# Moving the narrowing, bounds and splits of the second network's weights one stage ahead

## The chip, the cores and the metric

One core of a Trainium2 chip. The metric is the device time in microseconds (us) of one execution of the whole program, the median of several runs. Engines are called as the profile calls them: PE (TensorE matmuls), PEld (its weight loads), DVE (VectorE), ACT (ScalarE), POOL (GpSimd), SP (SyncE, which issues all the DMAs).

## The reference

Attention whose mask allows only pairs of query and key that fall to the same centroid, then two feed-forward networks on 1536 tokens of 512 features:

```python
h = np.maximum(x @ w1[e], 0.0); out += p[:, e:e + 1] * (h @ w2[e])   # 4 experts, 512 -> 1024 -> 512
h = x @ w_in; g = np.maximum(0.01 * h, h); out = g @ w_out           # 512 -> 2048 -> 512
```

The weights of the experts are float32. Those of the second network (w_in, w_out) come as float64.

## The kernel before

After attention the two networks are done in 24 chunks of 256 hidden columns, here called stages 0 to 23: stages 0 to 15 are the experts (N1 = 16), 16 to 23 the second network. A stage has two phases. The **product phase** makes h = x @ w1 for its 256 columns, applies the activation and splits h in two (hhi by ACT, hlo = g - hhi by POOL). The **output phase** makes h @ w2 in twelve **tiles** of six matmuls (emit_y1 or emit_y2), each into a PSUM bank of its own; DVE adds each tile to the accumulator. Every fp32 matmul is done as three fp16 ones on a high and a low part (hi·hi, hi·lo, lo·hi).

Stages 0 to 2 and 16 to 18 (PLAIN) do the product phase as six blocks of twelve matmuls. The others use seven products of half-size blocks in place of eight (emit_seven); for that, sums of the four blocks of w1 (tile `sums`, fp32, made by POOL, split into shi and slo) and sums of blocks of x are kept. In emit_seven DVE's additions (`plus`) stand between products that use the same PSUM bank: the last product adds onto bank d only after DVE has read d for c22.

Each weight chunk goes this way, w1 as part 0, w2 as part 1:

- **load**: SP moves it to raw12[part] (float32), or to raw64[part] for the second network (one buffer for each part).
- **narrow** (float64 only): five steps that build a float32 in raw12[part]; step 1 is an Abs on ACT, steps 2 to 5 are bit operations on DVE (L244, L247, L250, L253).
- **peak** (L216): ACT takes the largest absolute value of each partition. **peak_across** (L220): one small PE matmul into a PSUM bank brings the 128 values together. **peak_top** (L224 and `power`): DVE reduces them and makes a power of two. **out_scale** (L232) makes the factor for the output.
- **split** (weights_split): ACT scales raw12[part] in place (L267) and makes the high half (L260); POOL makes the low half in two instructions (L263).

raw12, w1hi/w1lo, w2hi/w2lo, raw64, sums, shi/slo are single buffers. Order on each engine is the order of emission (a manual schedule); each engine works through its queue in order, and waits between engines follow from the tiles that instructions read and write. Lists of small steps (`steps`, `later`, `late`) are spread over the blocks, products and tiles of a stage by popping a few after each.

In before, narrowing of w2 for stage c+1 starts with step 1 at the end of stage c's product phase (`late`, or the head of the output phase), steps 2 to 5 run between the first tiles of the output phase, and the peak after them. Its peak_across, peak_top and split run in the middle of the next stage's product phase. For w1 of stage c+1, steps 2 to 5 and the peak run in stage c's product phase, peak_across after tile 1, and peak_top and the split some tiles later. Bank 0 takes the peak_across of w1 after tile 1 and is wanted again by tile 6 (y_bank).

Stage 15 and 16 are the seam: stage 15's output phase also brings x for the second network into range (turn_sum, turn_max, turn_scale, turn_split: ACT and DVE), and stage 15 narrows both weights of stage 16. Attention ends with a list of actions sorted by a due time in sixths of a head (`at(when, fn)`); PEAK_AT holds the due times of the peaks of stage 0's two weights, FILL those of h products of stage 0 that are done early. `big()` hands out three PSUM tiles of two banks in turn.

Of the kernel before, what the change touches and what calls it, by code (L numbers as in the profile page):

```python
# [52 lines left out]
NORM_LAST = (6.49, 6.57)  # L53
PHI_LAST = ((0, 2, 4), (0, 2, 4))
SPLIT_AT = (2.3, 3.6, 5.3)
PEAK_AT = ((4.6, 7.2), (18.1, 19.0))
FILL = ((0, 0, 1.07), (0, 6, 1.08), (0, 12, 6.38), (0, 18, 6.39), (1, 0, 9.94), (1, 6, 10.27), (1, 12, 10.27))

BIG = float(2 ** 60)
# [17 lines left out]
def attention_moe_kernel(  # L77
# [13 lines left out]
    nc = tc.nc  # L91
# [120 lines left out]
        )  # L212
        nc.vector.reciprocal(out=t[:, 3:4], in_=t[:, 2:3])

    def peak(part):
        nc.scalar.activation(out=junk, in_=raw12[part].rearrange("p a b -> p (a b)"), func=AF.Abs, accum_out=pb16[part])  # L216

    def peak_across(part, ps):
        spread[part] = ps
# [16 lines left out]
    def weights_narrow(c, part):  # L236

        w = raw64[part].rearrange("p k (f t) -> p k f t", t=2)
        low, high = w[:, :, :, 0], w[:, :, :, 1]
        f = raw12[part]  # L240
        fi = f.bitcast(I32)
        return [
            lambda: nc.scalar.activation(out=f, in_=high.bitcast(F32), func=AF.Abs),
            lambda: nc.vector.tensor_scalar(  # L244
                out=f, in0=f, scalar1=F64_LEAST, scalar2=F64_MOST, op0=ALU.max, op1=ALU.min,
            ),
            lambda: nc.vector.tensor_scalar(  # L247
                out=fi, in0=fi, scalar1=3, scalar2=0x3FFFFFFF, op0=ALU.logical_shift_left, op1=ALU.bitwise_and,
            ),
            lambda: nc.vector.scalar_tensor_tensor(  # L250
                out=fi, in0=high, scalar=-0x40000000, in1=fi, op0=ALU.bitwise_and, op1=ALU.bitwise_or,
            ),
            lambda: nc.vector.scalar_tensor_tensor(  # L253
                out=fi, in0=low, scalar=29, in1=fi, op0=ALU.logical_shift_right, op1=ALU.bitwise_or,
            ),
        ]
# [7 lines left out]

    def weights_split(c, part, lo_engine=None):
        hi, lo = (w1s, w2s)[part][0]
        nc.scalar.activation(out=raw12[part], in_=raw12[part], func=AF.Copy, scale=pk[part][:, c % 2, 3:4])  # L267
        if lo_engine:
            split(hi, lo, raw12[part], lo_engine)
        else:  # L270
            split_halves(hi, lo, raw12[part])
# [564 lines left out]
        weights_load(0, 1)  # L836

    def peak_early(part):
        peak_across(part, big())
        peak_top(0, part)  # L840

    def split_early(n):
# [14 lines left out]
    def at(when, fn, *args):  # L857
        line.append((when, len(line), fn, args))
# [73 lines left out]
        at(when, warm, 1)  # L932
    at(J * (NH - 3) + 0.5, open_early)
    for part in range(2):
        at(J * (NH - 3) + PEAK_AT[part][0], peak, part)
        at(J * (NH - 3) + PEAK_AT[part][1], peak_early, part)
    for n in range(3):
        at(J * (NH - 2) + SPLIT_AT[n], split_early, n - 1)
# [128 lines left out]
                    like(ps, rhs), lhsT=w[:, k, fs], rhs=rhs, start=k + i == 0, stop=k == KC - 1 and i == 2,  # L1067
                )

    def emit_seven(c, steps):  # L1070

        w = w1s[0]
        a11, a12, a21, a22 = [
# [48 lines left out]
        for m in some_b:  # L1122
            product(z[m, "a"], a11, x11, m)
            nc.scalar.activation(out=u2[m], in_=z[m, "a"], func=AF.Copy)
        if not is_wide(c):
            weights_split(c, 1)
            out_scale(c)
        some()
        if c >= N1:
            plain_b(0)  # L1130
# [1 line left out]
        for m in some_b:  # L1132
            product(z[m, "b"], s2, t2, m)
            plus(u2[m], z[m, "b"], u2[m])
        if is_wide(c):
            peak_across(1, bank(7))
            peak_top(c, 1)
            weights_split(c, 1)
            out_scale(c)
        some()  # L1140
        for m in some_b:
            product(z[m, "a"], a12, x21, m, False)
# [11 lines left out]
        for m in some_b:  # L1154
            product(z[m, "e"], a22, t4, m)
            plus(z[m, "e"], z[m, "e"], u3[m])
            if m == A and c < N1:
                done(m, 1, 0, z[m, "e"])
            product(z[m, "d"], s1, t1, m)
            plus(c22[m], z[m, "d"], u3[m])  # L1160
        done(B if c < N1 else A, 1, 0, z[B if c < N1 else A, "e"])
        some()
        h_act(c, g, g, pbuf[0][:, 0, HT:HT + 512])
        split(hbuf[0][0][:, 1, HT:HT + 512], hbuf[0][1][:, 1, HT:HT + 512], g, nc.gpsimd)
        if c < N1:
            done(B, 1, 1, c22[B])
        else:
            plain_b(1)
        for m in some_b:
            product(z[m, "d"], s4, x22, m, False)  # L1170
            plus(z[m, "d"], z[m, "d"], u2[m])
            done(m, 0, 1, z[m, "d"])

    def emit_y1(c, i):

# [91 lines left out]
    for c in range(NCH):  # L1267
# [2 lines left out]
        steps, left, late = [], [], []  # L1270
        if more and is_wide(c + 1):
            narrow = [[] if c + 1 == N1 else weights_narrow(c + 1, n) for n in range(2)]
            if c == N1:
                steps.append(narrow[0][0])
            steps += narrow[0][1:]
            if c + 2 < NCH:
                steps.append(lambda: weights_load(c + 2, 0))
            steps.append(lambda: peak(0))
            if c + 1 == N1:
                steps += weights_narrow(N1, 1)  # L1280
            else:
                late.append(narrow[1][0])
        elif more:
            steps += [lambda: peak(0), lambda: weights_load(c + 1, 1)]
        if c in PLAIN:
            if not is_wide(c):
                weights_split(c, 1, nc.vector if c == 0 else None)
                out_scale(c)
            if c == N1:
                sums_left = turn_sums()  # L1290
                quota = [0, 0, 7, 0, 3, 3]
            if c == 0:
                sums_left = input_sums()
                quota = [0, 3, 7, 0, 5, 3]
            n = quota.pop(0)
            slots = mixed(sums_left[:n], steps) + late
            sums_left = sums_left[n:]
            if c == N1:
                turn_max(1)
                for k in range(KC):  # L1300
                    turn_split(1, k)
            blocks = [(u, f) for u in range(2 if c == 0 else 0, NU) for f in range(NF)]
            for n, (u, f) in enumerate(blocks):
                if c > 0 and c != N1:
                    ps = bank(BANKS[u][f])
                    plain(c, u, f, ps)
                elif f == 0:
                    both_ps = [bank(BANKS[u][f]) for f in range(NF)]
                    for k in range(KC):
                        for g in range(NF):  # L1310
                            plain(c, u, g, both_ps[g], [k])
                if c == 0 or c == N1:
                    ps = both_ps[f]
                h_whole(c, f, ps, 512 * u, hl=[tokens(x[:, f], c, u, True) for x in hbuf[0]])
                if c == N1 and (u, f) == (0, 1):
                    turn_across(1, bank(1))
                    turn_scale(1)
                    for k in range(KC):
                        turn_split(2, k)
                if is_wide(c) and (u, f) == (0, 1):  # L1320
                    peak_across(1, bank(6))
                    peak_top(c, 1)
                    weights_split(c, 1)
                    out_scale(c)
                if c == N1 and n < 2:
                    continue
                for _ in range(-(-len(slots) // (len(blocks) - n))):
                    slots.pop(0)()
        else:
            emit_seven(c, steps)  # L1330
            left = steps + late

        steps, later = left, []
        if c in PLAIN:
# [1 line left out]
            later, sums_left = sums_left[:n], sums_left[n:]  # L1336
        if more:
            if not is_wide(c + 1):
                later.insert(0, lambda: peak(1))
            else:  # L1340
                if c + 1 == N1:
                    steps.append(lambda: peak(1))
                else:
                    later += narrow[1][1:] + [lambda: peak(1)]
                if c + 2 < NCH:
                    later.append(lambda: weights_load(c + 2, 1))
            if L1_POINT(c):
                steps.append(lambda: weights_split(c + 1, 0))
            else:
                steps += [None, None, lambda: (peak_top(c + 1, 0), weights_split(c + 1, 0))]  # L1350
            if c + 1 not in PLAIN:
                steps += weights_sums()
            if c + 2 < NCH and not is_wide(c + 2):
                steps.append(lambda: weights_load(c + 2, 0))
# [9 lines left out]
        for i in range(NTILE):  # L1364
            (emit_y1 if c < N1 else emit_y2)(c, i)
            if i == 1 and more and not L1_POINT(c):
                peak_across(0, bank(0))
            if i == 8 and more and not is_wide(c + 1):
                peak_across(1, bank(7))
                steps.append(lambda: peak_top(c + 1, 1))  # L1370
            for _ in range(2 if c == N1 - 1 else -(-len(steps) // (NTILE - i))):
                step = steps.pop(0) if steps else None
                if step:
                    step()
        if c >= N1 and c + 2 < NCH:
            weights_narrow(c + 2, 0)[0]()


# [30 lines left out]
```

## Time and profile before

| | |
|---|---|
| median of 3 runs | 1002.84 us (1002.62 to 1002.92) |
| the profiled execution | 1002.35 us, of which the span from first to last instruction is 1000.6 |
| mean granted TensorE clock | 0.988 |
| PE busy | 957.6 us, 96% of the span |
| DVE, ACT, POOL busy | 730.5 (73%), 517.0 (52%), 534.3 (53%) |
| chain that ended last | PE 76%, DVE 11%, ACT 7%, POOL 3% |

A row of a timeline is: start, duration, engine, line, operation, output <- inputs with shapes, count, and in brackets how long the engine was idle before it and what ended that. A granted clock of 1.00 is full speed.

### The profile page before, as it was taken

How to read it: one execution, taken by the hardware profiler on the slowest of the kernel's cores; microseconds unless marked ns; L12 is line 12 of the kernel's file. 1: busy time of each engine (PE TensorE's matmuls, PEld its weight loads, DVE VectorE, ACT ScalarE, POOL GpSimd, SP SyncE). 2: the span in 40 equal slices, each digit the busy share in tenths (PEclk: the TensorE clock that was granted, in tenths of full speed). 3: DMA queues.
4: the chain of work that ended last, by engine and by line, in shares of the span. 5: the costliest groups of instructions: out<-in, count | busy, mean ns of one | idle time of the engine just before them, and what ended most of it. 6: DMA issues, size and time to landing. Idle time of an engine off the chain costs nothing.

```text
span 1000.6 us, 16132 instructions
## 1 busy us (share of the span) xinstructions
PE 957.6 (96%) x6347; PEld 547.9 (55%) x6380; DVE 730.5 (73%) x1264; ACT 517.0 (52%) x731; POOL 534.3 (53%) x444
## 2 busy tenths in 40 slices
PE   8899999997999999999999999999897999999998
PEld 5688888876444555555555555555443444434443
DVE  7988998887586767666666666667767967666654
ACT  3678877785443533443443444344573565455542
POOL 4477777760254656554565654455423746454543
PEclk9999999999999999999999999999899999999999
DMA  7875666430011031011301102131102122121103
GB/s 170 199 165 120 147 136 140 105 102 23 22 43 42 22 74 43 22 43 43 74 22 43 43 22 74 43 126 36 50 1 84 43 85 84 43 84 42 43 1 127
DMA packets 59540, 70.80 MB, mean 71 GB/s; under 512 B 25060, under 2 KB 42088, under 8 KB 59464
## 3 DMA queue, kind: packets, MB, share of 16 engines
q1 hardware_dynamic: 59464, 69.77, 26.4%
q8 instruction: 50, 0.82, 0.4%
q14 instruction: 26, 0.21, 0.1%
HBM read 46.19 MB, written 3.17 MB: 49 GB/s over the span
## 4 chain that ended last, share of the span: by engine, by line
PE 76%; DVE 11%; ACT 7%; POOL 3%; issue 2%; DMA 0%; DVEq 0%; ACTq 0%; POOLq 0%
PE z L1055 19%; PE z L1185 8%; PE z L1186 8%; PE z L1187 7%; PE z L1066 6%; PE z L1242 3%; PE z L1243 3%; PE z L1244 3%; PE big L510 3%; PE big L545 3%; PE big L546 2%; DVE m L514 2%; PE z L1114 2%; PE small L571 1%; PE small L572 1%
## 5 line engine op out<-in xcount | busy, mean ns | idle before, releaser
L141 POOL TENSOR_TENSOR hlo<-g,hhi 128x512 bf16<-128x512 f32 x140 | 175.9, 1272 | 131.8 <-ACT hhi L140 131.8
L1195 DVE SCALAR_TENSOR_TENSOR acc<-z,outer,acc 128x512 f32<-128x512 f32 x180 | 134.2, 749 | 75.2 <-PE z L1187 75.2
L559 POOL TENSOR_TENSOR plo<-p,phi 128x768 f16<-128x768 f32 x84 | 138.0, 1654 | 71.3 <-ACT phi L558 43.2
L1185 PE MATMUL z<-hhi,w2hi 128*128 128x512 f16 x384 | 145.8, 380 | 2.4 <-DVE pk L224 0.8
L140 ACT ACTIVATE hhi<-g 128x512 f16<-128x512 f32 x140 | 86.7, 628 | 116.4 <-DVE g L789 114.9
L1186 PE MATMUL z<-hhi,w2lo 128*128 128x512 f16 x384 | 145.8, 380 | 0.8 <-DVE w2lo L141 0.8
L1187 PE MATMUL z<-hlo,w2hi 128*128 128x512 bf16 x353 | 134.0, 380 | 0.0
L263 POOL TENSOR_TENSOR w2lo<-w2raw,w2hi 128x512 f16<-128x512 f32 x46 | 56.6, 1251 | 113.6 <-ACT w2hi L260 113.0
L514 DVE TENSOR_REDUCE m<-big 128x1 f32<-128x768 f32 x96 | 89.8, 950 | 14.5 <-PE big L510 14.2
L548 ACT ACTIVATE p<-big 128x768 f32<-128x768 f32 x96 | 77.4, 808 | 37.3 <-PE big L546 31.3
L263 POOL TENSOR_TENSOR w1lo<-w1raw,w1hi 128x512 f16<-128x512 f32 x46 | 56.1, 1241 | 75.3 <-ACT w1hi L260 48.9
L1242 PE MATMUL z<-w2hi,hhi 128*128 128x512 f16 x192 | 75.4, 393 | 7.3 <-DVE pk L224 7.3
L1251 DVE SCALAR_TENSOR_TENSOR accn<-z,outer,accn 128x512 f32<-128x512 f32 x84 | 61.1, 745 | 27.0 <-PE z L1244 27.0
L1066 PE MATMUL z<-xx,w1hi 128*128 128x512 f16 x256 | 76.3, 379 | 0.3 <-DVE xx L613 0.3
L1243 PE MATMUL z<-w2lo,hhi 128*128 128x512 f16 x192 | 75.4, 393 | 1.1 <-POOL w2lo L263 1.1
L1244 PE MATMUL z<-w2hi,hlo 128*128 128x512 f16 x192 | 75.3, 392 | 0.0
L545 PE MATMUL big<-qka 128*128 128x512 f32 x192 | 70.9, 370 | 2.9 <-DVE m L514 1.8
L1055 PEld LDWEIGHTS <-shi 128*128 128x128 f16 x496 | 48.8, 98 | 41.7 <-issue 5.9
L789 DVE SCALAR_TENSOR_TENSOR g<-z,pb 128x512 f32<-128x512 f32 x92 | 52.4, 576 | 20.1 <-PE z L1055 10.2
L1055 PE MATMUL z<-xx,shi 128*128 128x512 f16 (+1 forms) x248 | 62.7, 341 | 3.9 <-DVE g L1094 3.9
L1094 DVE TENSOR_TENSOR part<-z,part 128x512 f32<-128x512 f32 (+1 forms) x62 | 34.8, 578 | 41.3 <-PE z L1055 28.1
L573 PE MATMUL small<-vt,plo 128*128 128x65 f16 x576 | 61.0, 192 | 2.9 <-DVE plo L559 2.0
(238 smaller groups left out, 2263.8 us busy)
## 6 DMA issues: line engine op xcount, KB each, us to landing
qkb<-pair SPq DMA_DIRECT2D x32, 384.0 KB
w1raw<-in_moe_w_dram SPq DMA_DIRECT2D x16, 512.0 KB
w2raw<-in_moe_w_dram SPq DMA_DIRECT2D x16, 512.0 KB
w1raw<-in_moe_w_in_dram SPq DMA_DIRECT2D x8, 1024.0 KB
w2raw<-in_moe_w_out_dram SPq DMA_DIRECT2D x8, 1024.0 KB
qka<-pair SPq DMA_DIRECT2D x16, 384.0 KB
vraw<-in_v_dram SPq DMA_DIRECT2D x16, 192.0 KB
pb<-pe_rows SPq DMA_DIRECT2D x4, 768.0 KB
```

The costliest lines, as they stand in the source:

```text
L141: lo_engine.tensor_tensor(out=lo, in0=src, in1=as_read(hi), op=ALU.subtract)
L263: nc.gpsimd.tensor_tensor(out=lo[:, x], in0=src[:, x], in1=hi[:, x], op=ALU.subtract)
L514: nc.vector.tensor_reduce(out=m_t[t][:, j:j + 1], in_=ps[:, 0:S], op=ALU.max, axis=AX.X)
L559: (nc.vector if plo_on_vector else nc.gpsimd).tensor_tensor(out=plo, in0=p, in1=phi, op=ALU.subtract)
L1055: nc.tensor.matmul(ps, lhsT=w[i][:, k, :], rhs=x[j][:, k, sub], start=first and k + i + j == 0, stop=k == 1 and i == 1, skip_group_check=True,
L1066: nc.tensor.matmul(like(ps, rhs), lhsT=w[:, k, fs], rhs=rhs, start=k + i == 0, stop=k == KC - 1 and i == 2,)
L1185: nc.tensor.matmul(out, lhsT=whi[:, f, ks], rhs=h, start=f == 0, stop=False)
L1186: nc.tensor.matmul(out, lhsT=wlo[:, f, ks], rhs=h, start=False, stop=False)
L1187: nc.tensor.matmul(out, lhsT=whi[:, f, ks], rhs=l, start=False, stop=f == NF - 1)
L1195: nc.vector.scalar_tensor_tensor(out=a, in0=out, scalar=by, in1=a, op0=ALU.mult, op1=ALU.add)
L1242: nc.tensor.matmul(ps, lhsT=hi[:, f, ts], rhs=whi[:, f, :], start=f == 0, stop=False)
L1243: nc.tensor.matmul(ps, lhsT=hi[:, f, ts], rhs=wlo[:, f, :], start=False, stop=False)
```

## The change

- Due time of the peak matmul of stage 0's w2: 21.0 in place of 19.0; it uses the PSUM tile small0 in place of the next big tile.
- w2 of stage 16 is narrowed into `sums`; its peak is taken there, and its scaling writes raw12[1] from there.
- In stages 16 to 22 all five narrowing steps of the next w2 are in the product phase (`late`); its peak follows tile 1 of the output phase, its peak_across tile 8 (tile 5 in stage 15). Its split stands at the head of the next stage: in emit_seven after the first product, in stages 17 and 18 before the blocks, in stage 16 behind the second turn_split.
- peak_top and split of the next w1 follow peak_across directly, after tile 1.
- Narrowing steps 1 to 3 of w1 of stage 17 move to tiles 7 and 11 of stage 15. The peak of w1 comes before the load of the next w1.
- One of the block sums of x moves from stage 0's output phase to stage 1 (`quota`).

```diff
-PEAK_AT = ((4.6, 7.2), (18.1, 19.0))
+PEAK_AT = ((4.6, 7.2), (18.1, 21.0))
...
+    def narrowed(c, part):
+
+        return sums.rearrange("p (a e) b c -> p a (e b c)", a=2) if is_wide(c) and (c, part) == (N1, 1) else raw12[part]
...
     def weights_split(c, part, lo_engine=None):
         hi, lo = (w1s, w2s)[part][0]
-        nc.scalar.activation(out=raw12[part], in_=raw12[part], func=AF.Copy, scale=pk[part][:, c % 2, 3:4])
+        src = narrowed(c, part) if c else raw12[part]
+        nc.scalar.activation(out=raw12[part], in_=src, func=AF.Copy, scale=pk[part][:, c % 2, 3:4])
...
     def peak_early(part):
-        peak_across(part, big())
+        peak_across(part, small(0) if part else big())
         peak_top(0, part)
...
-    def emit_seven(c, steps):
+    def emit_seven(c, steps, late):
...
         for m in some_b:
             product(z[m, "a"], a11, x11, m)
             nc.scalar.activation(out=u2[m], in_=z[m, "a"], func=AF.Copy)
-        if not is_wide(c):
-            weights_split(c, 1)
-            out_scale(c)
+        weights_split(c, 1)
+        out_scale(c)
         some()
...
             product(z[m, "b"], s2, t2, m)
             plus(u2[m], z[m, "b"], u2[m])
-        if is_wide(c):
-            peak_across(1, bank(7))
-            peak_top(c, 1)
-            weights_split(c, 1)
-            out_scale(c)
         some()
...
             plus(c22[m], z[m, "d"], u3[m])
+        if late:
+            late[0]()
         done(B if c < N1 else A, 1, 0, z[B if c < N1 else A, "e"])
         some()
         h_act(c, g, g, pbuf[0][:, 0, HT:HT + 512])
         split(hbuf[0][0][:, 1, HT:HT + 512], hbuf[0][1][:, 1, HT:HT + 512], g, nc.gpsimd)
+        for step in late[1:3]:
+            step()
...
             done(m, 0, 1, z[m, "d"])
+        for step in late[3:]:
+            step()
...
             narrow = [[] if c + 1 == N1 else weights_narrow(c + 1, n) for n in range(2)]
-            if c == N1:
-                steps.append(narrow[0][0])
-            steps += narrow[0][1:]
-            if c + 2 < NCH:
-                steps.append(lambda: weights_load(c + 2, 0))
-            steps.append(lambda: peak(0))
+            load = [lambda: weights_load(c + 2, 0)] if c + 2 < NCH else []
             if c + 1 == N1:
-                steps += weights_narrow(N1, 1)
+                two = weights_narrow(N1, 1)
+                steps += [two[0], lambda: peak(c + 1, 0)] + load + two[1:]
             else:
-                late.append(narrow[1][0])
+                steps += narrow[0][3 if c == N1 else 1:] + [lambda: peak(c + 1, 0)] + load
+                late = narrow[1]
...
-                quota = [0, 3, 7, 0, 5, 3]
+                quota = [0, 2, 7, 1, 5, 3]
             n = quota.pop(0)
-            slots = mixed(sums_left[:n], steps) + late
+            slots = mixed(sums_left[:n], steps)
+            slots[len(slots) // 2:len(slots) // 2] = late[:1]
+            slots += late[1:]
             sums_left = sums_left[n:]
             if c == N1:
                 turn_max(1)
                 for k in range(KC):
                     turn_split(1, k)
+                weights_split(c, 1)
...
-                if is_wide(c) and (u, f) == (0, 1):
-                    peak_across(1, bank(6))
-                    peak_top(c, 1)
-                    weights_split(c, 1)
                     out_scale(c)
...
-                    later += narrow[1][1:] + [lambda: peak(1)]
+                    later.insert(0, lambda: peak(c + 1, 1))
...
-                steps += [None, None, lambda: (peak_top(c + 1, 0), weights_split(c + 1, 0))]
+                steps.insert(0, None)
...
             if i == 1 and more and not L1_POINT(c):
                 peak_across(0, bank(0))
-            if i == 8 and more and not is_wide(c + 1):
+                peak_top(c + 1, 0)
+                weights_split(c + 1, 0)
+            if i == (5 if c == N1 - 1 else 8) and more:
                 peak_across(1, bank(7))
                 steps.append(lambda: peak_top(c + 1, 1))
...
+            if c == N1 - 1 and is_wide(N1 + 1):
+                ahead = weights_narrow(N1 + 1, 0)
+                if i == 7:
+                    ahead[0]()
+                if i == 11:
+                    ahead[1]()
+                    ahead[2]()
```

## Rows read from the trace of the kernel before

**Rows 1.** Windows of stages 16, 17, 19, 22: us, busy (PE PEld DVE ACT POOL), clock, DMA.

```profile
730.62:771.22 40.60, 33.53 (x149) 14.63 (x148) 29.73 (x48) 25.77 (x42) 15.15 (x10) 0.96 0.12 36
771.22:802.41 31.19, 31.19 (x147) 14.19 (x146) 27.50 (x35) 17.91 (x24) 19.26 (x10) 1.00 0.21 68
833.60:867.56 33.96, 31.86 (x142) 13.97 (x140) 21.73 (x37) 19.58 (x28) 17.56 (x18) 0.95 0.28 93
935.49:966.73 31.24, 30.18 (x141) 13.54 (x140) 21.44 (x35) 15.58 (x23) 16.23 (x16) 1.00 0.00 1
```

**Rows 2.** PE's waits in the whole span, by releaser: total us, times, longest.

```profile
PE z L1242 <- DVE pk L224: 7.3, 4, 2.1
PE z L220 <- ACT junk L216: 5.6, 1, 5.6
PE z L1055 <- DVE g L1094: 3.9, 1, 3.9
...
PE big L220 <- ACT junk L216: 2.5, 1, 2.5
...
PE z L1243 <- POOL w2lo L263: 1.1, 2, 0.8
...
PE z L1185 <- DVE pk L224: 0.8, 1, 0.8
```

**Rows 3.** Windows of PE alone: length, busy, granted clock, DMA.

```profile
240.90:244.10 3.20, 3.19 (x9) 0.50 0.00 0
710.06:715.20 5.14, 5.14 (x16) 0.50 0.33 84
756.60:759.70 3.10, 3.10 (x9) 0.52 0.95 309
858.20:862.00 3.80, 3.80 (x11) 0.55 0.25 68
955.90:959.00 3.10, 2.04 (x10) 1.00 0.00 0
```

**Rows 4.** Timeline of DVE at the end of attention.

```profile
240.81 1.83 DVE L559 TENSOR_TENSOR plo<-p,phi 128x768 f16<-128x768 f32 x2
```

**Rows 5.** Timelines of ACT and DVE, product phase of stage 15.

```profile
700.04 1.04 ACT L216 ACTIVATE junk<-w1raw 128x1024 bf16<-128x1024 f32 x1
...
702.51 1.15 ACT L243 ACTIVATE w2raw<-w2raw 128x1024 f32<-128x1024 f32 x1 [1.34 <-POOL w2lo L263]
...
703.69 0.69 DVE L244 TENSOR_SCALAR w2raw<-w2raw 128x1024 f32<-128x1024 f32 x1 [4.70 <-ACT w2raw L243]
...
706.76 1.24 DVE L250 SCALAR_TENSOR_TENSOR w2raw<-w2raw,w2raw 128x1024 int32<-128x1024 int32 x1
```

**Rows 6.** Timelines of DVE and ACT, output phase of stage 15.

```profile
715.10 0.43 DVE L789 SCALAR_TENSOR_TENSOR g<-z,pb 128x256 f32<-128x256 f32 x1
...
719.96 0.75 DVE L1195 SCALAR_TENSOR_TENSOR acc<-z,outer,acc 128x512 f32<-128x512 f32 x1 [0.54 <-PE z L1187]
...
722.70 1.06 ACT L260 ACTIVATE w1hi<-w1raw 128x1024 f16<-128x1024 f32 x1
```

**Rows 7.** Chain that ended last, in order of time: start, us, what.

```profile
833.60 1.29 PE z L1055 x6
```

**Rows 8.** Timelines of POOL and DVE, apart and side by side, stages 14 and 16.

```profile
678.48 4.52 POOL L141 TENSOR_TENSOR hlo<-g,hhi 128x512 bf16<-128x512 f32 x4 [1.30 <-ACT hhi L140]
...
735.72 2.74 DVE L613 SCALAR_TENSOR_TENSOR xx<-acc,gx,xx 128x512 f16<-128x512 f32 x4 [0.46 <-ACT xx L612]
...
740.46 3.18 DVE L613 SCALAR_TENSOR_TENSOR xx<-acc,gx,xx 128x512 f16<-128x512 f32 x4 [1.18 <-ACT xx L612]
...
748.99 7.36 POOL L141 TENSOR_TENSOR hlo<-g,hhi 128x512 bf16<-128x512 f32 x4
...
751.18 2.06 DVE L250 SCALAR_TENSOR_TENSOR w1raw<-w1raw,w1raw 128x1024 int32<-128x1024 int32 x1
```

**Rows 9.** Timeline of POOL, product phase of stage 19.

```profile
842.70 2.53 POOL L263 TENSOR_TENSOR w2lo<-w2raw,w2hi 128x512 f16<-128x512 f32 x2 [2.68 <-ACT w2hi L260]
```

More of the change, by code (lines that the diff above doesn't have):

```diff
@@ L213, in power, with peak @@
         nc.vector.reciprocal(out=t[:, 3:4], in_=t[:, 2:3])
-    def peak(part):
-        nc.scalar.activation(out=junk, in_=raw12[part].rearrange("p a b -> p (a b)"), func=AF.Abs, accum_out=pb16[part])
+    def narrowed(c, part):
+        return sums.rearrange("p (a e) b c -> p a (e b c)", a=2) if is_wide(c) and (c, part) == (N1, 1) else raw12[part]
+    def peak(c, part):
+        src = narrowed(c, part) if c else raw12[part]
+        nc.scalar.activation(out=junk, in_=src.rearrange("p a b -> p (a b)"), func=AF.Abs, accum_out=pb16[part])
     def peak_across(part, ps):
@@ L239, in weights_narrow @@
         low, high = w[:, :, :, 0], w[:, :, :, 1]
-        f = raw12[part]
+        f = narrowed(c, part)
         fi = f.bitcast(I32)
@@ L266, in weights_split @@
         hi, lo = (w1s, w2s)[part][0]
-        nc.scalar.activation(out=raw12[part], in_=raw12[part], func=AF.Copy, scale=pk[part][:, c % 2, 3:4])
+        src = narrowed(c, part) if c else raw12[part]
+        nc.scalar.activation(out=raw12[part], in_=src, func=AF.Copy, scale=pk[part][:, c % 2, 3:4])
         if lo_engine:
@@ L934, in attention_moe_kernel @@
     for part in range(2):
-        at(J * (NH - 3) + PEAK_AT[part][0], peak, part)
+        at(J * (NH - 3) + PEAK_AT[part][0], peak, 0, part)
         at(J * (NH - 3) + PEAK_AT[part][1], peak_early, part)
@@ L1272, in attention_moe_kernel @@
             narrow = [[] if c + 1 == N1 else weights_narrow(c + 1, n) for n in range(2)]
-            if c == N1:
-                steps.append(narrow[0][0])
-            steps += narrow[0][1:]
-            if c + 2 < NCH:
-                steps.append(lambda: weights_load(c + 2, 0))
-            steps.append(lambda: peak(0))
+            load = [lambda: weights_load(c + 2, 0)] if c + 2 < NCH else []
             if c + 1 == N1:
-                steps += weights_narrow(N1, 1)
-            else:
-                late.append(narrow[1][0])
+                two = weights_narrow(N1, 1)
+                steps += [two[0], lambda: peak(c + 1, 0)] + load + two[1:]
+            else:
+                steps += narrow[0][3 if c == N1 else 1:] + [lambda: peak(c + 1, 0)] + load
+                late = narrow[1]
         elif more:
-            steps += [lambda: peak(0), lambda: weights_load(c + 1, 1)]
+            steps += [lambda: peak(c + 1, 0), lambda: weights_load(c + 1, 1)]
         if c in PLAIN:
-            if not is_wide(c):
+            if c != N1:
                 weights_split(c, 1, nc.vector if c == 0 else None)
@@ L1311, in attention_moe_kernel @@
                             plain(c, u, g, both_ps[g], [k])
[L1312 to L1315, printed above, removed]
+                if c == N1 and n == 0:
                     turn_across(1, bank(1))
@@ L1319, in attention_moe_kernel @@
                         turn_split(2, k)
-                if is_wide(c) and (u, f) == (0, 1):
-                    peak_across(1, bank(6))
-                    peak_top(c, 1)
-                    weights_split(c, 1)
                     out_scale(c)
+                if c == 0 or c == N1:
+                    ps = both_ps[f]
+                h_whole(c, f, ps, 512 * u, hl=[tokens(x[:, f], c, u, True) for x in hbuf[0]])
                 if c == N1 and n < 2:
@@ L1328, in attention_moe_kernel @@
                     slots.pop(0)()
+            left = []
         else:
-            emit_seven(c, steps)
-            left = steps + late
+            emit_seven(c, steps, late)
+            left = steps
         steps, later = left, []
@@ L1338, in attention_moe_kernel @@
             if not is_wide(c + 1):
-                later.insert(0, lambda: peak(1))
+                later.insert(0, lambda: peak(c + 1, 1))
             else:
                 if c + 1 == N1:
-                    steps.append(lambda: peak(1))
+                    steps.append(lambda: peak(c + 1, 1))
                 else:
-                    later += narrow[1][1:] + [lambda: peak(1)]
+                    later.insert(0, lambda: peak(c + 1, 1))
                 if c + 2 < NCH:
@@ L1374, in attention_moe_kernel @@
                     step()
-        if c >= N1 and c + 2 < NCH:
+            if c == N1 - 1 and is_wide(N1 + 1):
[5 more added lines that the diff above has]
+                    ahead[2]()
+        if c >= N1 and c + 2 < NCH and is_wide(c + 2):
             weights_narrow(c + 2, 0)[0]()
```

## The prediction

> **What bounds the kernel.** The table above says that PE is busy for 957.6 of 1000.6 us, so the time is PE's matmuls, PE's waits, and what the matmuls lose at a lower clock. I read the windows by stage first [rows 1]: stages 17 and 22 show PE busy all or nearly all the time, 31.19 of 31.19 and 30.18 of 31.24 us, and are the measure of an undisturbed stage; stages 16 and 19 are longer than PE's work in them. Then PE's waits by releaser [rows 2]: the six that touch this change sum to 7.3 + 5.6 + 3.9 + 2.5 + 1.1 + 0.8 = 21.2 us, and all name the peak, narrowing or splitting of weights, or DVE sums queued behind a narrowing step. Last, the granted clock behind those waits [rows 3]: it falls to its lower level (1.2 of 2.4 GHz) after the waits of 2 us and more, and stays at 1.00 after one of 1.06 us (955.90:959.00, PE busy 2.04 of 3.10). One minus the clock, times the stretch, is the loss: 1.6, 2.6, 1.5, and 1.7 in each of stages 19 to 21, which are alike: 10.8 us. So 32.0 us can be won at most, which would be 970.4 of the profiled execution's 1002.35.
>
> **What the change does to the count of work.** Nothing is added or removed: the same narrowings, peaks, splits and loads run, in another order, with one other buffer and one other PSUM tile. Every microsecond is a wait that goes or comes.
>
> **A. Hand-over from attention, and stage 0.** PE waited 2.5 us for the peak of the first w2 and then lost 1.6 to the clock [rows 2, 3]. The peak's matmul now stands behind twelve h products and three products with v. The h products take the next of the three big tiles, whose last reader, an exponential, is long done, so they start at once, 2.6 us of work at full clock. The v products then need the last plo, which DVE finishes at 240.81 + 1.83 = 242.64 [rows 4]; PE gets there at about 241.4 and waits 1.2. The shifted tiles also put the second block's h in the PSUM that stage 0 opens with: I allow 0.5 for it (0 to 1.4). 2.5 + 1.6 - 1.2 - 0.5 = 2.4. In stage 0 peak_top now follows tile 1 directly, so bank 0 is free for tile 6 and the 0.8 us wait goes. A gives 3.2 (1.0 to 4.9).
>
> **B. Stage 15.** Before, the first narrowing step of w2(16), the Abs on ACT, waited for POOL's split of the old weight in the same buffer and ended at 703.66; DVE, in order, stood behind it from 699.0 to 703.69, and the sums behind DVE's steps came late: the last product waited 3.9 us, to 710.06, then ran 5.1 us at half clock [rows 3, 5]. With the block-sum buffer the Abs takes the place of the peak at 700.04 and ends near 701.2, so DVE starts 2.45 sooner. The order on DVE from there to the c22 sum is unchanged, so PE resumes at 710.06 - 2.45 = 707.6; it is there at 706.2 and waits 1.4. That is nearer the 1.06 that left the clock alone than the 2 us that didn't: I take no loss (bound: the 2.6 stays). 3.9 + 2.6 - 1.4 = 5.1.
> Then a new wait. The peak of w2(16) must now be there after tile 5. DVE leaves the product phase 5.5 us after PE resumed (715.10 + 0.43 against 710.06), runs two accumulations and the scale chain, then ACT scales and splits w1: from an accumulation's start to the split's end is 719.96 to 723.76, 3.8; the extra accumulation is 0.7, the peak and its read-out 1.2 [rows 5, 6]. 5.5 + 0.7 + 3.8 + 1.2 = 11.2 after PE resumes. PE is at the end of tile 5 after 1.9 (the two last products) + 6 x 1.29 = 9.7, six matmuls of 512 columns taking 1.29 [rows 7]. So it waits about 1.4. B gives 3.7 (1.3 to 6.4). The Abs of w1(17) at tile 7 lies in ACT's idle time; the two DVE steps at tile 11 fall where DVE waits for ACT anyway: 0.
>
> **C. Stage 16.** Before: 1.1 for w2lo, 5.6 for the peak of w1(17), 1.5 of clock: 8.2 us [rows 2, 3]. Three of its five narrowing steps are now done in stage 15, and the split of w2(16) goes ahead of the blocks on ACT and POOL. DVE is free for steps 4 and 5 when the last splits of x end, at 740.46 + 3.18 = 743.6 in before's times, where step 4 began at 751.18 [rows 8]. Alone, two steps of 1.2 each and the peak would be done by about 747.5. PE asks for it two tiles into the output phase, 730.62 + 16.2 (six blocks of twelve matmuls, and 0.7 of small ones and waits) + 2.6 = 749.4: nothing would be left. But POOL is now busy in the same stretch. POOL's four subtractions took 4.52 us alone and 7.36 beside narrowing steps, one of which took 2.06 there and 1.24 alone; four x splits took 2.74 alone and 3.18 where they met POOL's for a moment [rows 5, 8]. That is taking turns, each waiting for the other. From 740.4 DVE has 5.0 us of such work (four x splits, two steps) and 0.4 that is free of POOL, and POOL has w2lo and three hlo to do all the while. Taking turns, the steps end at 740.4 + 2 x 5.0 + 0.4 = 750.8, the peak at 752.0; PE waits 2.6 and then loses 1.7 to the clock. C gives 8.2 - 4.3 = 3.9 (0.5, if POOL holds the steps another 3 us, to 8.2, if nothing is left). I take the 3.9, since each such DVE row beside POOL is stretched.
> The Trainium skill (SBUF — State Buffer, "Who interferes with whom") says that a VectorE instruction with two SBUF inputs and a GpSimd one that reads SBUF contend for a port pair, the later one blocking for the whole instruction; it speaks against packing narrowing beside POOL's splits. By it C is the 3.9 above; were the pair free, C would be 8.2. The stretched rows agree with it.
>
> **D. Stages 17 and 18.** DVE is busy 27.5 of 31.19 us in stage 17 already [rows 1]. Its product phase now also holds the four DVE steps of w2(18): eight steps and five block sums, 0.6 or 1.13 us apiece by their rows alone, 12.6 us, beside eight POOL subtractions of 1.13, 9.1 us. DVE starts 1.2 us into the stage, POOL 2.2; POOL's work is gone at 2.2 + 2 x 9.1 = 20.4, DVE's remaining 2.5 at 22.9. Two accumulations and the peak reduction free bank 0 at 24.5; tile 6 wants it at 15.5 + 7.8 = 23.3. Loss 1.2 (0 to 2.6). Stage 18 has fewer sums and no wait.
>
> **E. Stages 19 to 22.** Each has 30.2 us of PE work and took 33.96 three times and 31.24 once: 7.3 waits and 5.1 clock, 12.4 in all [rows 1 to 3]. The wait was at tile 6: bank 0 was still to be read by DVE's peak reduction, which stood behind narrowing steps of w2. Now two steps stand behind the c22 sum, in the product phase, two behind its last sum, and peak_top directly behind tile 1. The last sum ends 15.1 us into the stage; two steps taking turns with POOL's last hlo end at 18.9, two accumulations and the reduction at 20.5. Tile 6 wants bank 0 at 14.3 + 7.8 = 22.0: the cover is 1.5 us, and beyond it each microsecond counts in four stages. At the stage head ACT's scaling of w2 waits for peak_top behind the last accumulation, about 2.4 in; queued behind it are Prelu and hhi of the first blocks, whose consumers are the tiles from 14.3 on: hidden. E gives 12.4 (8.4, with a wait of 1.0 left in each, to 12.4). The loads of raw w1 and w2 move on SP by a step or a few tiles; each weight is used a stage later, and SP has nothing else there: 0.
>
> **Sum.** 3.2 + 3.7 + 3.9 - 1.2 + 12.4 = 22.0. The profiled execution would take 980.3; the median of the runs is 0.5 above it, so 980.8.
>
> **The rivals.** (1) Taking turns doesn't bite: nothing is left in C and D. 980.8 - 4.3 - 1.2 = 975.3, and 972.5 if the waits of 1.4 in stage 15 are hidden too. For it: DVE and POOL need not meet; against it: the stretched rows. Chance 0.25. (2) DVE is overcrowded in stages 19 to 22: steps end over 1.5 us later than I have them, and waits of 2.1 with 1.7 of clock come back in three of them: 980.8 + 11.4 = 992.2. For it: POOL works beside most steps; against it: DVE is busy 21.7 of 33.96 [rows 1]. Chance 0.13. (3) Slower: the Abs of the second weight on ACT, now ahead of the activation that the first output tiles need, is held by POOL's w2lo, which still reads the buffer. I have w2lo done 8 us into the stage and the Abs begun at 11; PE waits once w2lo ends later than 11.9, a microsecond for each in four stages. To lose more than 22 us it must end 5.5 us after that, at 17.4; before, it started late and ended 842.70 + 2.53 - 833.60 = 11.6 in [rows 9]. With 6 us: 1005. Chance 0.05. (4) The peaks were not what held PE, and the same waits move along to another tile: within 0.2% (2 us, about what a measurement can tell from no change). Chance 0.03. That leaves 0.54 for the forecast, whose own range is 976 to 986. The poor ends of A to E together give 994, the good ends 971; 972 to 990 leaves out most of (2), (3) and (4) and little of (1). Faster 0.92, same 0.03, slower 0.05.
>
> **What would show it.** After: the wait at the last product of stage 15 down to 1 to 2 us; one before tile 6 of stage 15 on the peak; PE's wait for the peak in stage 16 between 0 and 3 us; stages 19 to 22 within 0.3 us of 30.2 with the clock at 1.00. I am wrong if narrowing steps of w2 end after tile 3 in those stages, or if DVE's steps beside POOL are not stretched.

## The result and the profile after

The changed kernel takes 977.88 us (median of 6 runs, 976.73 to 978.09) against 1002.88 of the kernel before: a ratio of 0.9747, 95% interval 0.9734 to 0.9759. The forecast was 980.8 (972 to 990; own range 976 to 986). The profiled execution after took 978.03, its span 976.3 against 1000.6, so there are 24.3 us to place.

PE's waits of the profile after, by releaser: total, times, longest. Rows that the change does not touch are left out.

```profile
PE z L1061 <- DVE g L1100: 1.8, 1, 1.8
PE z L1072 <- DVE p L827: 1.4, 1, 1.4
...
PE z L1250 <- POOL hlo L141: 1.3, 1, 1.3
PE z L225 <- ACT junk L221: 1.2, 1, 1.2
...
PE z L225 <- DVE g L795: 0.8, 1, 0.8
```

Four of the six rows of [rows 2] have no successor: peak_top (7.3), w2lo (1.1), the first peak (2.5) and tile 6 (0.8). The 5.6 is now 1.2 and the 3.9 is 1.8. One more row of the kernel before has gone, a wait at an output tile of stage 0 that the six don't count:

```profile
PE z L1186 <- DVE w2lo L141: 0.8, 1, 0.8
```

Three rows are new: 1.4 at the start of stage 0 (L1072), 0.8 at a peak matmul in stage 15, 1.3 for an hlo in stage 16. The windows of stages 15, 16, 17, 19 and 22 after, as in [rows 1]:

```profile
692.02:725.17 33.15, 30.12 (x159) 15.26 (x159) 26.98 (x57) 19.72 (x36) 11.90 (x10) 1.00 0.19 64
725.17:760.28 35.11, 32.17 (x149) 14.12 (x148) 31.69 (x48) 25.81 (x42) 16.31 (x10) 1.00 0.18 60
760.28:791.65 31.37, 31.37 (x147) 14.13 (x146) 30.28 (x35) 17.99 (x24) 18.29 (x10) 1.00 0.21 68
822.84:852.74 29.90, 29.90 (x142) 13.64 (x140) 23.23 (x35) 16.86 (x25) 20.16 (x17) 1.00 0.23 71
912.53:942.43 29.90, 29.90 (x142) 13.64 (x140) 23.24 (x35) 16.41 (x24) 20.38 (x17) 1.00 0.00 1
```

The clock is 1.00 in all of them. The only fall of the profile after that PE works in lies in attention (windows of PE alone; one more lies in the last microsecond of the span, when PE has nothing left to do):

```profile
228.00:232.00 4.00, 1.46 (x22) 0.91 0.00 0
232.00:236.00 4.00, 4.00 (x28) 0.50 0.44 131
236.00:240.00 4.00, 4.00 (x46) 0.73 0.00 0
```

The table gives what each stage took in each profiled kernel, from its first product on PE to the next stage's, read from PE's timeline (stage 16 so ends some 0.2 us earlier than in the windows). "Stage 0 ends" is a time from the span's start and holds attention too.

| kernel | stage 0 ends | 15 | 16 | 17 | 19 to 22 | median us | ratio, 95% |
|---|---|---|---|---|---|---|---|
| before | 279.73 | 36.88 | 40.43 | 31.20 | 133.13 | 1002.88 | |
| after | 278.02 | 33.16 | 34.93 | 31.38 | 119.58 | 977.88 | 0.9747 (0.9734–0.9759) |
| e1_handover_alone | 277.36 | 36.80 | 40.40 | 31.19 | 133.12 | 999.89 | 0.9973 (0.9961–0.9985) |
| e2_peaktop_alone | 279.88 | 37.25 | 40.63 | 31.19 | 123.01 | 992.39 | 0.9905 (0.9883–0.9927) |
| e3_peaktop_back | 277.57 | 32.97 | 35.87 | 33.33 | 119.59 | 981.20 | 0.9795 (0.9771–0.9819) |
| e4_own_buffer | 276.67 | 36.08 | 34.93 | 31.36 | 119.58 | 980.71 | 0.9786 (0.9761–0.9810) |
| e5_lo_on_dve | 277.83 | 33.14 | 35.93 | 31.38 | 119.57 | 978.15 | 0.9748 (0.9729–0.9766) |
| e6_peak_later | 278.01 | 32.01 | 35.23 | 31.38 | 119.59 | 977.14 | 0.9735 (0.9720–0.9751) |
| e7_steps_later | 276.44 | 34.24 | 34.93 | 31.38 | 119.59 | 978.82 | 0.9753 (0.9738–0.9769) |
| e8_other_banks | 277.93 | 33.16 | 34.94 | 31.36 | 119.59 | 977.14 | 0.9739 (0.9723–0.9755) |
| e9_w2_steps_back | 279.60 | 32.02 | 33.99 | 32.21 | 119.58 | 978.29 | 0.9746 (0.9732–0.9761) |
| e10_next_big | 277.38 | 33.18 | 34.94 | 31.36 | 119.59 | 977.36 | 0.9745 (0.9729–0.9761) |
| e11_together | 276.79 | 31.99 | 33.99 | 32.19 | 119.59 | 976.26 | 0.9734 (0.9718–0.9751) |
| e12_steps_later | 276.36 | 32.35 | 34.94 | 31.38 | 119.58 | 975.74 | 0.9726 (0.9711–0.9740) |

The ratios are to runs of the kernel before beside each, whose medians were 1002.65 to 1003.26. One of e4's four runs took 2521.57 us, in the slow state, and is left out of its median. Each stage's time is that of one profiled execution.

From before to after: A 1.7, stage 15 3.7, stage 16 5.5, stage 17 -0.2, stages 19 to 22 13.5: before rounding 24.3, all of it. "Stage 0 ends" varies with the execution, by 3.2 us among kernels that are the same code up to there (276.36 in e12 to 279.60 in e9); the last section shows from where.

### The profile page after: what moved, and what is told of

It is laid out like the page before. It is cut to its first block, busy times and chain, and to the rows that moved or that the text cites. A ratio compares the mean times of both kernels' runs of the same rounds, so it can differ in the third digit from the quotient of the medians.

```text
span 976.3 us, 16148 instructions
## 1 busy us (share of the span) xinstructions
PE 948.7 (97%) x6347; PEld 547.8 (56%) x6380; DVE 746.8 (76%) x1264; ACT 517.1 (53%) x731; POOL 555.0 (57%) x444
## 4 chain that ended last, share of the span: by engine, by line
PE 84%; DVE 9%; ACT 2%; DMA 2%; issue 1%; POOL 1%; SPq 0%; DVEq 0%; ACTq 0%
PE z L1061 21%; PE z L1191 8%; PE z L1192 8%; PE z L1193 7%; PE z L1072 7%; PE z L1250 4%; PE z L1248 4%; PE z L1249 4%; PE big L516 3%; PE z L1120 3%; PE big L551 3%; PE big L552 2%; DVE m L520 2%; PE small L577 1%; PE small L578 1%
## 5 line engine op out<-in xcount | busy, mean ns | idle before, releaser
L141 POOL TENSOR_TENSOR hlo<-g,hhi 128x512 bf16<-128x512 f32 x140 | 195.7, 1417 | 98.2 <-ACT hhi L140 98.2
L1072 PE MATMUL z<-xx,w1hi 128*128 128x512 f16 x256 | 76.4, 379 | 1.7 <-DVE p L827 1.4
L1250 PE MATMUL z<-w2hi,hlo 128*128 128x512 f16 x192 | 72.8, 379 | 1.4 <-POOL hlo L141 1.3
L1248 PE MATMUL z<-w2hi,hhi 128*128 128x512 f16 x192 | 72.8, 379 | 0.0
L1249 PE MATMUL z<-w2lo,hhi 128*128 128x512 f16 x192 | 72.8, 379 | 0.0
L1193 PEld LDWEIGHTS <-w2hi 128*128 128x128 f16 x384 | 37.6, 98 | 45.3
```

Source lines behind the costliest of these rows:

```text
L141: lo_engine.tensor_tensor(out=lo, in0=src, in1=as_read(hi), op=ALU.subtract)
L1072: nc.tensor.matmul(like(ps, rhs), lhsT=w[:, k, fs], rhs=rhs, start=k + i == 0, stop=k == KC - 1 and i == 2,)
L1193: nc.tensor.matmul(out, lhsT=whi[:, f, ks], rhs=l, start=False, stop=f == NF - 1)
L1248: nc.tensor.matmul(ps, lhsT=hi[:, f, ts], rhs=whi[:, f, :], start=f == 0, stop=False)
L1249: nc.tensor.matmul(ps, lhsT=hi[:, f, ts], rhs=wlo[:, f, :], start=False, stop=False)
L1250: nc.tensor.matmul(ps, lhsT=lo[:, f, ts], rhs=whi[:, f, :], start=False, stop=f == NF - 1)
```

## The experiments

### The hand-over alone

```diff
-PEAK_AT = ((4.6, 7.2), (18.1, 19.0))
+PEAK_AT = ((4.6, 7.2), (18.1, 21.0))
-        peak_across(part, big())
+        peak_across(part, small(0) if part else big())
```

> The kernel before with the first w2's peak moved back behind the h products and into a small PSUM tile, and nothing else of the change. My part A without the 0.8 us of tile 6: 2.4 us, 1000.5. The trace of after showed 1.7 us for all of A, with a stretch of 6.4 us at half clock that before does not have: by that reading 0.9 us, 1002.0, with the half-clock stretch again at 231.6 to 238 us. Rival: the gain is given back whole by the wait at the first product of stage 0, 1002.9.

2.4 us on the trace (stage 0 ends at 277.36, not 279.73), 2.9 on the medians; every later stage is as before. The wait of 1.4 at the start of stage 0 and the 0.8 of tile 6 are there, the 0.8 for w2lo is not, and PE ran 232 to 236 us at 0.65 of full clock. The edit wins; the 1.4 is its own price.

### Which half of the edit frees stages 19 to 22

e2 is the kernel before with only this:

```diff
-                steps += [None, None, lambda: (peak_top(c + 1, 0), weights_split(c + 1, 0))]
+                steps += [None, None]
...
                 peak_across(0, bank(0))
+                peak_top(c + 1, 0)
+                weights_split(c + 1, 0)
```

e3 takes the same lines of the kernel after back to the list.

> The kernel before with peak_top and the split of the next w1 directly behind tile 1 in every stage, the narrowing of w2 left in the output phase. Theory P: the place of peak_top is what counts in stages 19 to 22, since only the first narrowing step stands ahead of it now; stages 19 to 22 take 29.9 to 30.3 us, and with the 0.8 of stage 0 the time is 988 to 990. Theory N: the narrowing of w2 had to leave the output phase; stages 19 to 21 keep over 1 us of wait and its clock loss, and the time is 995 or more.

> The kernel after with peak_top and the split of the next w1 back in the list of later steps, some two tiles later; the narrowing of w2 stays in the product phase. If either half of the edit is enough in stages 19 to 22, bank 0 is read some 21 us into each of them against 22.0 wanted, and only the 0.8 of stage 0 and about 1 us in stage 17 come back: 979 to 981. If peak_top's place is the needed half, 2 us and its clock come back in three or four stages: 986 to 990.

With peak_top alone early, 10.1 of the 13.5 us come; with the narrowing alone moved, all 13.5. DVE's timeline in stage 19 of e2, from tile 1 on:

```profile
855.27 0.28 DVE L224 TENSOR_REDUCE pk<-z 128x1 f32<-128x128 f32 x1
...
857.30 1.23 DVE L250 SCALAR_TENSOR_TENSOR w2raw<-w2raw,w2raw 128x1024 int32<-128x1024 int32 x1
858.43 1.41 DVE L1251 SCALAR_TENSOR_TENSOR accn<-z,outer,accn 128x512 f32<-128x512 f32 x2
859.75 2.09 DVE L253 SCALAR_TENSOR_TENSOR w2raw<-w2raw,w2raw 128x1024 int32<-128x1024 int32 x1
861.76 4.69 DVE L1251 SCALAR_TENSOR_TENSOR accn<-z,outer,accn 128x512 f32<-128x512 f32 x7
```

Bank 0 is read early, but the steps now hold the accumulations: PE waits 0.56 for one late in the output phase of each of three stages, far too little to touch the clock (the other half of the 1.1 us by which these stages exceed 29.9 shows in no wait). So each half removes the 2 us waits, and neither theory of e2 is whole. In e3, at 981.20 a little over the 979 to 981 of "either half is enough", the time comes back elsewhere: 0.9 in stage 0 (tile 6), 0.9 each in stage 1 (32.13, not 31.19) and stage 16, and 2.0 in stage 17, whose wait for peak_top is there again. The half that stages 19 to 22 could spare is needed by stage 17.

### The block-sum buffer

```diff
-        return sums.rearrange("p (a e) b c -> p a (e b c)", a=2) if is_wide(c) and (c, part) == (N1, 1) else raw12[part]
+        return raw12[part]
```

> The kernel after with the first wide w2 narrowed in the buffer of the old weight, as before. My part B: the Abs on ACT waits for the split of the old weight again, the last product of stage 15 for the sums, 3.9 us in place of 1.75 and 2.6 us of clock: 982.0 to 983.0. Rival: it was the new order of the steps and not the buffer: 977.9, stage 15 unchanged at 33.15 us.

Stage 15 takes 36.08, 2.9 more than after, the median 980.71: less than I expected, since the clock cost 1.7 here (0.56 in the window below, 0.87 in the three us behind it), not 2.6, and the 0.82 at bank 0 is not there. Timelines: the Abs on ACT after; the Abs, DVE's first step and PE's wait in e4; and the window of PE behind that wait:

```profile
698.32 1.12 ACT L248 ACTIVATE sums<-w2raw 128x1024 f32<-128x1024 f32 x1
```

```profile
699.44 1.13 ACT L248 ACTIVATE w2raw<-w2raw 128x1024 f32<-128x1024 f32 x1 [2.38 <-POOL w2lo L268]
...
700.61 0.69 DVE L249 TENSOR_SCALAR w2raw<-w2raw 128x1024 f32<-128x1024 f32 x1 [4.68 <-ACT w2raw L248]
...
706.98 0.67 PE L1061 MATMUL z<-xx,shi 128*128 128x512 f16 x2 [3.88 <-DVE g L1100]
```

```profile
707.00:710.00 3.00, 3.00 (x11) 0.56 0.02 5
```

ACT stands 2.38 us for POOL's split, DVE behind ACT, PE behind DVE. The buffer is worth 2.9 of stage 15's 3.7. The other 0.8 (36.88 to 36.08) is clock: the wait is the same 3.9 as before, but 1.7 us were lost behind it and not 2.6. Whether the new order of the steps or the execution made that difference is not shown.

### Where the waits of stage 15 go

e6 asks later for both peaks; e7 and e12 ask one tile later in stage 15 only and put two narrowing steps behind the c22 sum (`late = two[3:]`). In e7 steps 3 and 4 ran in exchanged order, so w2(16) holds other values there; e12 has the right order.

```diff
-            if i == 1 and more and not L1_POINT(c):
+            if i == (2 if c == N1 - 1 else 3 if c == N1 else 1) and more and not L1_POINT(c):
```

> The kernel after with the peak's matmul for w1(16) one tile later in stage 15 and that for w1(17) two tiles later in stage 16. Theory: the 0.82 us of stage 15 goes (stage 15 near 32.3), since bank 0 is free by then; in stage 16 the 1.19 of the peak goes, but the low halves of the last h blocks, which stand behind the same DVE steps, are no earlier: their wait grows from 1.27 to about 2.4, stage 16 stays at 34.9 or loses up to 1.5 more to the clock. Rival: the two waits of stage 16 are separate, and it takes 33.7.

> The kernel after with the last two narrowing steps of w2(16) put behind the c22 sum in stage 15, and the peak's matmul for w1(16) one tile later there. Theory: the 1.75 us at the last product is the narrowing step ahead of the sums on DVE (1.24 us); it falls to about 0.5, and part of it comes back behind the two steps on DVE, at the first output tiles or at the peak of w2(16): stage 15 takes 31.2 to 32.4 us in place of 33.16. Rival: the sums wait for something else, and the two steps now hold the h blocks instead: stage 15 at 33 us or more.

> The kernel after with the peak's matmul for w1(16) one tile later, and steps 4 and 5 of the narrowing of w2(16) behind the c22 sum of stage 15, in their right order. Theory: the wait of 1.75 us at the last product falls to about 0.5, and the step that was ahead of the sums now holds the last h blocks, so that bank 0 is read later: a wait of 1 to 2 us comes up there, and stage 15 takes 32.0 to 33.2 us, against 32.01 with the peak later alone. Rival: nothing comes back, 30.6 to 31.2.

The theories of e6 and e12 held; e7's forecast of 31.2 to 32.4 was missed. In e6 stage 15 is 1.15 shorter, and in stage 16 the peak's 1.19 went over to the h blocks (a row of 2.2 for hlo, one of 0.4 for g): 35.23. In e12 the 1.75 at the last product is gone, and PE stands 1.95 at the next thing that DVE owes it:

```profile
710.44 0.22 PE L225 MATMUL z<-identb,pb 128*128 128x128 bf16 x1 [1.95 <-DVE g L795]
```

That is stage 15 in 32.35, no better than e6's 32.01; in e7, with one more step behind the sum, this wait is 2.3, the clock behind it 0.54 (711.5 to 715.2 us, 1.7 us lost), and the stage 34.24.

### DVE and POOL in stage 16

```diff
-                weights_split(c, 1)
+                weights_split(c, 1, nc.vector)
```

> The kernel after with the low half of w2(16) computed on DVE instead of POOL at the start of stage 16. Theory: DVE and POOL take turns; with POOL idle then, the four x splits that took 4.99 us beside POOL's subtraction take 2.7 to 3.4, which pays for the 1.1 to 1.3 that DVE takes over; the peak of w1(17) is ready 0.5 to 1.2 us sooner, and stage 16 takes 33.7 to 34.4 us in place of 34.93. Rival: the splits are slow for a reason of their own; they stay at 4.5 to 5 us, DVE is 1.2 us later, and stage 16 takes 36 us or more with the clock loss.

Four x splits and the narrowing steps behind them on DVE's timeline, and POOL's beside it, after and then in e5:

```profile
734.85 4.99 DVE L619 SCALAR_TENSOR_TENSOR xx<-acc,gx,xx 128x512 f16<-128x512 f32 x4 [1.01 <-ACT xx L618]
...
740.13 1.82 DVE L255 SCALAR_TENSOR_TENSOR w1raw<-w1raw,w1raw 128x1024 int32<-128x1024 int32 x1
741.99 2.06 DVE L258 SCALAR_TENSOR_TENSOR w1raw<-w1raw,w1raw 128x1024 int32<-128x1024 int32 x1
743.97 1.64 DVE L249 TENSOR_SCALAR w2raw<-w2raw 128x1024 f32<-128x1024 f32 x1
...
734.35 2.73 POOL L268 TENSOR_TENSOR w2lo<-w2raw,w2hi 128x512 f16<-128x512 f32 x2 [16.25 <-ACT w2hi L265]
737.94 7.12 POOL L141 TENSOR_TENSOR hlo<-g,hhi 128x512 bf16<-128x512 f32 x4 [0.86 <-ACT hhi L140]
```

```profile
734.04 1.23 DVE L141 TENSOR_TENSOR w2lo<-w2raw,w2hi 128x1024 f16<-128x1024 f32 x1 [1.23 <-ACT w2hi L140]
...
736.83 2.74 DVE L619 SCALAR_TENSOR_TENSOR xx<-acc,gx,xx 128x512 f16<-128x512 f32 x4 [0.74 <-ACT xx L618]
...
739.86 1.21 DVE L255 SCALAR_TENSOR_TENSOR w1raw<-w1raw,w1raw 128x1024 int32<-128x1024 int32 x1
741.10 2.06 DVE L258 SCALAR_TENSOR_TENSOR w1raw<-w1raw,w1raw 128x1024 int32<-128x1024 int32 x1
...
739.91 11.60 POOL L141 TENSOR_TENSOR hlo<-g,hhi 128x512 bf16<-128x512 f32 x6 [22.01 <-ACT hhi L140]
```

The mechanism shows cleanly: the same four splits take 2.74 with POOL idle and 4.99 beside it, a narrowing step 1.21 where it began ahead of POOL's subtraction and 1.82 to 2.06 where POOL was at work, and a step of 0.69 alone took 1.64. The experiment's forecast of the stage was a miss all the same, 35.93 and not 33.7 to 34.4: DVE stood 1.23 for w2hi before it could begin, so the splits started 2 us later, PE waited 1.5 in sum for x, and POOL then had all six hlo beside the narrowing steps (11.60).

e9 leaves w2lo on POOL and takes four narrowing steps of w2(17) out of the product phase, with e6's peaks:

```diff
-            slots += late[1:]
+            slots += late[1:] if c != N1 else []
...
+        if c == N1:
+            steps = [None] * 3 + late[1:] + [lambda: peak(c + 1, 1), lambda: weights_load(c + 2, 1)] + [None] * 3
```

> The kernel after with the two peaks of stages 15 and 16 asked for later, as in the run before this one, and with four narrowing steps of w2(17) put back from stage 16's product phase into its output phase, from tile 3 on. Theory: the last waits of stage 16, 0.96 and 1.27 us for low halves of h, come from POOL's subtractions standing beside those DVE steps (4.19 us for two that take 2.3 alone); they fall to 0.5 or less in sum, stage 16 takes 33.0 to 33.6 us in place of 35.23, and the time is 974.5 to 976. Rival: POOL is slow beside any DVE work there, or the steps hold the accumulations of the output phase: stage 16 at 34.5 or more.

The waits for hlo went as the theory has it, but stage 16 took 33.99, above the 33.0 to 33.6 expected, and stage 17 became 0.8 us longer. PE's waits of e9 in those two stages:

```profile
PE z L225 <- ACT junk L221: 2.0, 1, 2.0
PE z L1248 <- DVE pk L229: 0.8, 1, 0.8
```

The steps, now late, make the peak of w2(17) late (1.98 us at tile 8), and the shift brings back a wait for peak_top in stage 17. Over both stages 66.2 us, against 66.3 after and 66.6 in e6, whose peaks it has; and as stage 0 ended late in e9's profiled execution, at 279.60, that took 978.32. The median is 978.29, not 974.5 to 976.

### The start of stage 0

e8: other banks for stage 0's first products (`bank(BANKS[u if c else 0][f])`, and tiles 0 and 3 change banks). e10: one more line, `at(J * (NH - 3) + 19.0, big)`. e11: e9 and e10 together.

> The kernel after with stage 0's first products in two other PSUM banks, and the first output tile of stage 0 in the bank freed by that. Theory: the 1.4 us at the start of stage 0 is the wait for DVE to read the second h block out of the PSUM that the first products want; with other banks it goes, and attention's end plus stage 0 is 1.2 to 1.4 us shorter. Rival: the products wait for the readers of the last transposed tile, or the output tiles of stage 0 for h, and nothing is won.

> The kernel after with one turn of the three big PSUM tiles passed over at the place where the kernel before had the peak's matmul, so that the second h block is again in the same tile as before. Theory: the 1.4 us at the start of stage 0 is the wait for the last reader of the PSUM pool that holds the h block, whichever of its banks is asked for; it goes, and stage 0 ends 1.4 us sooner, at 275.0 to 276.7. Rival: the h products wait 1 us or more for the tile that is now theirs, and nothing is won.

> The two kernels of this call that undo waits, together: peaks later, narrowing steps of w2(17) back in the output phase, and one turn of the big tiles passed over. If their gains are separate, 1.1 (stage 15), 1.7 (stage 16) and 1.4 (stage 0) come off 977.9: 973.7, within 972.5 and 975.0. If the gain at stage 0 is eaten by the clock or the h products: 975 to 976.

In e8 the wait stayed at 1.38 to the hundredth: the bank is not what it hangs on. In e10 it is gone, so it is the tile that holds the second h block, or the pool it is in; 0.8 of it came back at once at an output tile:

```profile
261.82 0.39 PE L1193 MATMUL z<-hhi,w2lo 128*128 128x512 f16 x1 [0.80 <-DVE w2lo L141]
```

Stage 0 ended at 277.38, against 278.02 after, which had a like stretch at half clock: 0.6 won, not 1.4; my range for it was missed. e11's stages 15 to 17 are those of e9 to 0.03 us, and the wait of 1.4 is gone as in e10. But the gains of e9 and e10 were smaller than the 4.2 us that its forecast added up: its median is 976.26, not 972.5 to 975.0, with an interval that overlaps that of after. No version has an interval clear of the changed kernel's; e12 is the fastest, and of its lead on the trace (973.8 of span against 976.3) 1.7 is where stage 0 ended, which the code of e12 does not touch, and 0.8 is stage 15.

## Why the prediction was right, point by point

The profiled execution is 24.3 us shorter, not 22.0: A is 1.5 below its term, C 1.6, D 1.0 and E 1.1 above theirs.

- **What bounds the kernel.** Right: all 24.3 us are waits and the clock behind them; PE has 6347 matmuls in both. The 32.0 us "at most" were no true bound: they left out the 0.8 for w2lo in stage 0, and an undisturbed stage is shorter than the 30.2 taken.
- **A, 3.2 forecast, 1.7 here.** The mechanism was right, and the sum too where the execution had neither a late start nor a stretch at half clock (see the last section), but by errors that cancel, which is luck. The 1.4 at the start of stage 0 is the upper end of my bound (I took 0.5). The 1.2 for the last plo is 0.36 and 0.60 in e12, which kept its clock there (PE's timeline below). And the 0.8 for w2lo, which I had not counted, went; without the 1.4 it is back (e10). 2.5 + 1.6 + 0.8 + 0.8 - 1.4 - 0.36 - 0.60 = 3.3, and e7 and e12, the same code up to here, ended stage 0 3.3 and 3.4 us sooner than before. In the execution after, the stretch at half clock from 231 to 238 us took the other 1.7; no term of mine stands for it. Five executions of the same code that had such a stretch, or a late start, or both, give 0.1 to 3.1.

```profile
241.82 0.20 PE L579 MATMUL small<-vt,plo 128*128 128x65 f16 x1 [0.36 <-DVE plo L565]
...
242.69 0.20 PE L579 MATMUL small<-vt,plo 128*128 128x65 f16 x1 [0.60 <-DVE plo L565]
```

- **B, 3.7 forecast, 3.7.** The wait at the last product is 1.75 (forecast 1.4) and cost no clock, as taken. The wait that I put before tile 6, on the peak of w2(16), did not come: 0.82 came instead at the peak's matmul for w1(16), because bank 0 was still being read by the last h on DVE. The sum was right for two wrong halves, which is in part luck; e12 shows a reason why such halves offset each other: there DVE, relieved ahead of one matmul, made PE stand at the next.
- **C, 3.9 forecast, 5.5.** The mechanism was right, the size off. I counted strict turns, 2 x 5.0 + 0.4 from the x splits to the end of step 5; the rows above give 744.05 - 734.85 = 9.2. PE asked when I said, and waited 1.19, not 2.6, with the clock at 1.00, not 1.7 lost. Against that the sum lacked the 1.27 for hlo: I followed DVE's side of the turns and not POOL's, whose subtractions were stretched too (7.12 for four, 4.52 alone [rows 8]). Rival (1), that turns don't bite, is refuted by e5's rows.
- The Trainium skill (SBUF — State Buffer, "Who interferes with whom") has the engine that issues first hold the shared port pair for its whole instruction while the other is blocked. The direction agrees; by an estimate from rows, strict turns would need more time than was taken: from 737.94 to 745.06 POOL did 4.5 us and DVE some 4.3 of work by their durations alone, 8.8 in 7.1 (DVE's: the last of the x splits 1.0, out_scale 0.4, two steps of 1.2, and part of a third, 0.5).
- **D, -1.2 forecast, -0.2.** DVE's steps in stage 17 ended 21.8 into the stage (forecast 22.9), for the same reason as in C, and the cover held.
- **E, 12.4 forecast, 13.5.** All waits and clock losses went; an undisturbed stage is 29.9, not 30.2. DVE's timeline in stage 19 after:

```profile
834.67 0.69 DVE L249 TENSOR_SCALAR w2raw<-w2raw 128x1024 f32<-128x1024 f32 x1 [0.26 <-ACT w2raw L248]
...
839.35 2.06 DVE L258 SCALAR_TENSOR_TENSOR w2raw<-w2raw,w2raw 128x1024 int32<-128x1024 int32 x1
841.33 1.40 DVE L1257 SCALAR_TENSOR_TENSOR accn<-z,outer,accn 128x512 f32<-128x512 f32 x2
842.65 0.28 DVE L229 TENSOR_REDUCE pk<-z 128x1 f32<-128x128 f32 x1
```

The steps end 18.6 into the stage (forecast 18.9), the reduction at 20.1 (20.5), tile 6 wants it at 22.0. Rivals (2) and (3) did not occur: POOL's w2lo ended 6.4 into stage 19 (829.24).

## What to carry to other kernels

An in-order engine that is behind pays at the next point where the bound engine asks it for something: here moving one step or one peak moved waits of 1 to 2 us from matmul to matmul, and only spreading the work over another stage, or into a buffer that is free, made them go. Before counting on such a move, list what that engine owes next, on both sides where two engines slow each other. Where an edit has two halves, try each alone in every stage that it touches: the half that looked spare in four stages carried a fifth.

## What the hardware showed

Waits of 1.75 (after), 1.95 (e12), 1.97 (e3, stage 17) and 1.98 us (e9) left the clock at 1.00 in the windows behind them; 2.30 (e7) brought it to 0.54 and 3.88 (e4) to 0.56. In [rows 2, 3] waits of 2.1 us were followed by a fall.

The same scattered idle time at 228 to 232 us, PE busy 1.46 of 4.00, was followed by nearly 7 us at half clock after, by some 3 in e4 and by none in e12 or before, with the same instructions up to there. Up to 230 us DVE and ACT of both kernels are within 0.12 us of e12's; behind the stretch stage 0 is 1.7 us later than e12's after, and 0.3 in e4. What decides it is open.

The executions also differ at their start. PE's first six matmuls on qraw, after and then in e6:

```profile
6.36 0.87 PE L336 MATMUL big<-ident,qraw 128*128 128x128 f32 x6
```

```profile
6.36 1.55 PE L336 MATMUL big<-ident,qraw 128*128 128x128 f32 x6
```

They took 1.54 or 1.55 us in e2, e5, e6, e8 and e9, and 0.87 or 0.88 in the other nine, before included. e5, e6 and e8 show no fall of the clock in attention and still ended stage 0 at 277.8 to 278.0: they are 1.4 to 1.7 us behind e12 from the first 11 us on. Why those six matmuls are slow there is not shown; the windows give a clock of 1.00 for that time too. The start and the stretch together make the 3.2 us between e12 and e9, so a difference of 1 or 2 us between two kernels' times says little here until the two profiles have been compared stage by stage.
